# Sixteen visits outside the loop instead of 24, all score maxima inside it, and 24 products held for the end

## The chip, the cores and the metric

The kernel runs on one core of a Trainium2 chip. A core has a matmul engine (TensorE, PE in the profile, with its weight loads as PEld), a vector engine (DVE), an activation engine (ACT), a general engine (POOL) and an engine that mostly issues DMAs (SP). Each works through its own instructions in order; they meet at semaphores. The metric is the device time of one execution in microseconds (us).

## What is computed

The reference mixes an attention block and a token-mixing MLP with a gate for each token. S is 2048 tokens, D is 640, there are 32 heads of 20 that share one key and one value head, and F is 1728.

```python
q, k, v = x @ wq, x @ wk, x @ wv                 # q: 32 heads of 20, k and v: one head of 20
p = softmax(q @ k.T * 20 ** -0.5)                # for each head, over 2048 keys
a = (p @ v, heads side by side) @ wo             # 2048 x 640
b = (gelu(layernorm(x).T @ w1 + b1) @ w2 + b2).T # 2048 x 640
g = sigmoid(x @ gate_w)
out = g * a + (1 - g) * b
```

## The kernel before

**Units.** Queries are cut into 4 blocks of 512 and heads into 8 groups of 4, which gives 32 query tiles, n = 0 to 31. Keys are cut into 16 blocks of 128. One query tile with one key block is a unit, and there are 512 of them, in order of n. A unit has four score products of 128 keys by 512 queries (`qk`, L688), each followed by an exponential on ACT (L700), and then its visit: the four exponentials are multiplied with v into one PSUM bank (`pv_mm`, L721, 32 columns of the array for each head, in two passes, so eight instructions a unit). The array is used as two row halves, b = 0 and b = 1, that run side by side as two lanes: two heads of a unit belong to each half.

**Maxima.** The softmax needs the largest score of each query. For each query tile, 64 further products of 128 queries by 512 keys (`ms_next`, L506, 32 for each half) are reduced to maxima by DVE (L514). When a tile has all 64, DVE merges them (L536), POOL negates and splits them into a high and a low part (L532 to L534), DVE turns them (L541), SP writes them to DRAM (`store_max`, L542), and four DMAs (`fetch_max`, L549, two for each half) put them as two extra rows into the query tile, so that `qk` of that tile subtracts the maximum by itself. The first `qk` of a tile has to wait for these rows. In a step of the loop, `fetch_at` issues them beside the visit of the key block kb = 11 of the tile before.

**The loop.** `n_st` = (512 - TAIL) / 2 = 244 steps. Step j issues, for one half h = j % 2, the eight score products of four units; some maxima (`wants[j]`); on the other half the next batch of other work; and then, as a burst, the visits of units 2j - 2 and 2j - 1. After the burst ACT copies the sum out of its bank (`collect`, L742) and POOL adds it to `osum` (L743). The other work is, in this order, MLP part one, MLP part two, and from step 200 on the output product of a block of 128 tokens (`a_jobs`, L961): for each half of the 640 columns, 5 pieces of the contraction times 3 terms (high by high, low by high, high by low) times 2 row halves, 15 products to a step, four steps to a block. Blocks st = 0 to 10 are done so.

**Scale and store of a query tile.** After its last visit, eight small stages (`norm_steps`, L747) are taken one to a step by `settle`: write the row sums, read them back, reciprocal on DVE (L760), write it (L763), read it back broadcast (four DMAs, L767), scale on POOL (L770), split on POOL (L773, L774), and store the rows to `o_scr` (`put_o`, eight DMAs, L733).

**The tail.** The last 24 units run in 12 stretches (`stretch`), two units each. A stretch has eight score products (four to each half), 16 maxima in all in the first three stretches, and a share of the waiting output products (`tail_job`, L910), in an order found by a random search over a model of the lanes (`best_order`, `trial`); then two visits that add up in one PSUM bank over a whole query tile (`o_bank`), with no collect. The waiting products are all of block 11 (`jobs[0]`, 60 products), the first 384 rows of blocks 12 to 15 (36 products each) and rows 384 to 560 of these (9 for each half of the columns), as a second sum with an addition of its own; three of these eight halves are held (`held`). Each sum ends in a DVE operation that scales by g and adds (L922). Query tile 30 is closed in the tail by `turned_steps` (L784 on).

**The end.** Rows 560 to 640 belong to the heads of query tile 31, which is known only after the last visit. While DVE and ACT normalize it (`last_half`, L812 to L817), PE does the held products with all 128 rows (L1424, 18 of them). Then 24 products with the last 80 rows of wo (`final`, L1402) finish the eight results of blocks 12 to 15, which DVE (L1411) or ACT and POOL (L1414, L1415) scale and add, and two queues store (L1437). The 80 rows of wo come through `last_wo` (a POOL memset, L982, then four DMAs, L985) and `split_last` (POOL).

All DMAs but the last two are issued by SP in program order; an SP instruction that waits holds up those behind it. The same holds for POOL's queue.

Of the kernel before, what the change touches and what calls it, by code (L numbers as in the profile page):

```python
# [10 lines left out]
F32 = mybir.dt.float32  # L11
# [7 lines left out]
P = 128  # L19
# [12 lines left out]
TAIL = 24  # L32
# [7 lines left out]
def mix_kernel(ctx: ExitStack, tc: tile.TileContext, A_x, A_wq, A_wk, A_wv, A_wo,  # L40
# [826 lines left out]
    whole = []  # L867
    tail = [[], []]
    loaded = []
    CUT = 3 * P  # L870
# [5 lines left out]
    def room(i):  # L876
        t, at = (u0, 3 * D * i) if i < 4 else (slot[0], 3 * D * (i - 4))
        return (t[:, at:at + 2 * D].rearrange("p (j c q) -> p j c q", j=2, q=P), f32(t[:, at + 2 * D:at + 3 * D]))

    def tail_load(i):  # L880
        if i < len(jobs):
            st, r0, r1 = jobs[i]
            cols = slice(st * P, (st + 1) * P)
            oT, yt = room(i)
            c0, c1 = r0 // P, r1 // P
            for j in range(2):
                nc.sync.dma_start(out=f32(oT[:, j, c0:c1]),
                                  in_=o_scr[j, r0:c1 * P, cols].rearrange("(c p) s -> p c s", p=P))
                if r1 > c1 * P:
                    nc.sync.dma_start(out=f32(oT[:r1 - c1 * P, j, c1]), in_=o_scr[j, c1 * P:r1, cols])  # L890
            if r0 == 0:
                nc.sync.dma_start(out=yt, in_=y_scr[cols, :])
            loaded.append(i)

    def tail_job(n):
        st, r0, r1 = jobs[n]
        oT, yt = room(n)
        acc, at, ready = {}, {}, []

        def mm(c, k, d, h, first, last):  # L900
            if first:
                i = at[d, h] = busy[h] = next_free()
                while any(k == i for _, k, _ in reduces):
                    reduces.pop(0)[2]()
                acc[d, h] = bank(i)
                free[i] = float("inf")
            o, w = ((oT[:, 0], wo_hi), (oT[:, 1], wo_hi), (oT[:, 0], wo_lo))[k]
            r = slice(64 * h, min(r1 - c * P, 64 * h + 64))
            region = [("x", at[d, h])]
            touch(nc.tensor.matmul(acc[d, h][:, :HD2], o[r, c, :], w[r, c, d * HD2:(d + 1) * HD2],  # L910
                                   start=first, stop=last), writes=region)
            if last:
                ends = lane[h] + 0.15
                while reduces and reduces[0][0] < ends:
                    reduces.pop(0)[2]()
                free[at[d, h]] = spend("dve", 0.48, ends) + 0.24
                sl = slice(d * HD2, (d + 1) * HD2)
                if st not in parts:
                    parts[st] = fin.tile([P, D], F32, name="yo") if r1 == D else spare_row(st)
                add = parts[st] if d in ready or r0 else yt  # L920
                ready.append(d)
                touch(nc.vector.scalar_tensor_tensor(parts[st][:, sl], acc[d, h][:, :HD2], g_col[:, st:st + 1],  # L922
                                                     add[:, sl], op0=ALU.mult, op1=ALU.add), region)
                if len(ready) == 4:
                    if r1 - r0 == D:
                        whole.append(lambda: nc.sync.dma_start(out=y_out[st * P:(st + 1) * P, :], in_=parts[st]))

        for h in range(2):
            ck = [(c, k) for c in range(r0 // P, DC) if r1 - c * P > 64 * h for k in range(3)]
            for d in range(2):  # L930
                if r0 and (st, d) in held:
                    continue
                for i, (c, k) in enumerate(ck):
                    step = lambda a=(c, k, d, h, i == 0, i == len(ck) - 1): mm(*a)
                    tail[h].append((n, ("a" if i == 0 else "e" if i == len(ck) - 1 else "f", step)))
# [104 lines left out]
    aj = [a_jobs(st) for st in range(NS - 5)]  # L1040
# [23 lines left out]
    for i, j in enumerate((221, 241, 242, 243, 243)):  # L1064
        ph[j][1].append(lambda i=i: tail_load(i))
# [131 lines left out]
    for i, (st, r0, _) in enumerate(jobs):  # L1197
        tail_job(i)
# [18 lines left out]
    left, n = 64 * NU - 16 - sum(given) - sum(wants[:at]), n_st - at  # L1217
    wants[at:] = sorted(left * (i + 1) // n - left * i // n for i in range(n))
    assert sum(given) + sum(wants[:n_st - 8]) >= 64 * (NU - 1)
    owed = 0  # L1220
    for j in range(n_st):
# [47 lines left out]
    assert sum(given) == 64 * NU - 16 and not follow  # L1269
# [18 lines left out]
    def trial(kinds, prefer):  # L1288
        line, new, banks_at, held_at = list(lane), list(fresh), list(free), dict(busy)
        dve, act, now, out = clock["dve"], clock["act"], state["at"], []  # L1290
        left = [list(x) for x in kinds]
        while any(left):
            options = []
            for k in range(4):
                if left[k]:
                    at = max(line[k % 2] + W_US * new[k % 2], now)
                    if left[k][0] in "sma":
                        at = max(at, min(banks_at))
                    options.append((at + prefer(k, left), k, at))
            _, k, at = min(options)  # L1300
            kind, h, now = left[k].pop(0), k % 2, at
            new[h] = False
            line[h] = at + (X_US if k < 2 else F_US)
            i = min(range(len(banks_at)), key=lambda i: banks_at[i])
            if kind == "s":
                act = max(act, at + SEEN_US) + EACH["act"][0]
                banks_at[i] = act - EACH["act"][0] + EACH["act"][1]
            elif kind == "m":
                dve = max(dve, at + SEEN_US) + EACH["dve"][0]
                banks_at[i] = dve - EACH["dve"][0] + EACH["dve"][1]  # L1310
            elif kind == "a":
                held_at[h], banks_at[i] = i, float("inf")
            elif kind == "e":
                dve = max(dve, line[h] + 0.15) + 0.48
                banks_at[held_at[h]] = dve + 0.24
            out.append(k)
        end = max(max(line), now + LAST_US - FIRST_US)
        late = sum(max(0.0, t - end - 2.0) for t in banks_at if t < float("inf"))
        return end + 0.3 * late, out

    def best_order(tiles, lanes, i):
# [3 lines left out]
        for _ in range(400):  # L1325
            w = [rng.uniform(-0.4, 0.4) for _ in range(4)]
            z = rng.uniform(0.0, 0.4)
            score = trial(kinds, lambda k, left: w[k] + rng.uniform(0.0, z))
            if best is None or score < best:
                best = score  # L1330
        return best[1]

    busy = {}

    def stretch(i):
# [3 lines left out]
        for b in range(2):  # L1339
# [3 lines left out]
            ms = [("m", ms_next(b)) for _ in range((3, 3, 2)[i] if i < 3 else 0)]  # L1343
            lanes[b] = tail_take(b, math.ceil(len(tail[b]) / (TAIL // 2 - i)))
            tiles[b] = ms + ss if i == 2 else [x for n in range(4) for x in ss[n:n + 1] + ms[n:n + 1]]
# [6 lines left out]
        if i == 2:  # L1352
            for f in ms_done():
                f()
            store_max(NU - 1)
            stores.pop()()
            fetch_max(NU - 1)
        if i > 2 and whole:
            whole.pop()()
        settle()  # L1360
        settle()
        pop_chain()
        if i in (7, 8):
            tail_load(2 * i - 9)
            tail_load(2 * i - 8)
# [12 lines left out]
    assert not tail[0] and not tail[1] and not any(later) and not whole  # L1378
# [80 lines left out]
```

## Time and profile before

| | |
|---|---|
| time, median of 3 runs | 1618.53 us (1618.27 to 1618.7) |
| time of the profiled execution | 1618.5 us |
| its span, first to last instruction | 1616.5 us |
| around the span | 2.0 us |
| mean granted TensorE clock | 0.999 |
| PE busy | 1608.8 us, 100% |
| DVE busy | 1383.9 us, 86% |
| ACT busy | 1261.1 us, 78% |
| POOL busy | 841.1 us, 52% |

Times inside the trace count from the start of the span. A matmul's busy time overlaps with that of its neighbours, so a full PE row does not say that PE is at its peak; the distance between the starts of neighbouring instructions does. A visit shows as a group of L721 instructions, so the distance from one group of 16 to the next is the length of a step or a stretch.

### The profile page before, as it was taken

The page shows a single profiled execution, that of the slowest core. Times are in us where ns is not written, and L with a number is a line of the kernel's source. Part 1 is how long each engine was busy: PE and PEld are TensorE (multiplying, and loading weights), DVE is VectorE, ACT ScalarE, POOL GpSimd, SP SyncE. Part 2 cuts the span into 40 slices and gives each one's busy share as a digit, 9 for nine tenths or more (in the row PEclk, how much of TensorE's full clock was granted, in tenths as well). Part 3 has the DMA queues.
Part 4 walks back from the last instruction along what each step waited for, and adds up shares of the span by engine and source line. Part 5 has one row for each costly group of instructions (what it writes and reads, how often), then busy time and mean ns, then how long its engine had stood idle before and what let it go on. Part 6 is the DMA issues. An engine that isn't in the chain of part 4 may idle for free.

```text
span 1616.5 us, 39520 instructions
## 1 busy us (share of the span) xinstructions
PE 1608.8 (100%) x14868; PEld 1123.3 (69%) x14868; DVE 1383.9 (86%) x2629; ACT 1261.1 (78%) x2350; POOL 841.1 (52%) x927
## 2 busy tenths in 40 slices
PE   9999999999999999999999999999999999999998
PEld 7899876776776776666666666666666666666665
DVE  6689899999999999888888888888888886567754
ACT  4545677777777778878888788887888879999976
POOL 6567766777787776554554334444444433333321
PEclk9999999999999999999999999999999999999999
DMA  7665322232222232222212121112221113333221
GB/s 215 206 168 144 87 66 73 61 77 69 69 70 74 53 76 63 74 68 69 69 47 64 35 61 54 58 54 60 61 60 47 54 37 112 103 115 98 85 83 59
DMA packets 180308, 129.27 MB, mean 80 GB/s; under 512 B 41585, under 2 KB 150030, under 8 KB 180118
## 3 DMA queue, kind: packets, MB, share of 16 engines
q1 hardware_dynamic: 179830, 126.43, 27.7%
q8 instruction: 117, 1.92, 0.5%
q14 instruction: 73, 0.60, 0.1%
q10 hardware_dynamic: 288, 0.33, 0.1%
HBM read 93.57 MB, written 32.15 MB: 78 GB/s over the span
## 4 chain that ended last, share of the span: by engine, by line
PE 98%; POOL 0%; DVE 0%; DMA 0%; issue 0%; ACT 0%; POOLq 0%; SPq 0%; DVEq 0%
PE xs L721 29%; PE xs L688 18%; PE xs L506 18%; PE g L836 11%; PE g L1008 7%; PE pp L302 4%; PE pu L633 4%; PE g L961 3%; PE xs L910 1%; PE x L506 1%; PE pt L294 0%; PE pp L366 0%; PE xs L1424 0%; PE pp L191 0%; PE g L688 0%
## 5 line engine op out<-in xcount | busy, mean ns | idle before, releaser
L514 DVE TENSOR_REDUCE mp<-xs 128x1 f32<-128x512 f32 x1943 | 1196.9, 684 | 154.7 <-PE xs L688 78.4
L700 ACT ACTIVATE p<-xs 128x512 f32<-128x512 f32 (+1 forms) x1834 | 1011.7, 680 | 10.9 <-PE xs L688 6.4
L743 POOL TENSOR_TENSOR osum<-osum,part 128x512 f32<-128x512 f32 x212 | 274.2, 1294 | 604.8 <-ACT part L742 597.9
L721 PE MATMUL xs<-p,v_sb 128*32 128x512 f32 x4096 | 492.3, 598 | 0.0
L688 PE MATMUL xs<-q,kst 62*128 62x512 f32 x1339 | 476.2, 417 | 1.3 <-ACT p L700 1.3
L506 PE MATMUL xs<-kst,q 60*128 60x512 f32 x1242 | 437.4, 416 | 0.0
L688 PEld LDWEIGHTS xs<-q,kst 62*128 62x128 f32 x1339 | 235.9, 185 | 74.6 <-DVE mp L514 52.3
L742 ACT ACTIVATE part<-xs 128x512 f32<-128x512 f32 x212 | 126.8, 598 | 199.6 <-PE xs L721 197.3
L1008 PE MATMUL g<-slot,w 64*128 64x320 f32 x1728 | 266.8, 306 | 0.0
L721 PEld LDWEIGHTS xs<-p,v_sb 128*32 128x32 f32 x4096 | 106.9, 109 | 225.5 <-issue 161.0
L506 PEld LDWEIGHTS xs<-kst,q 60*128 60x128 f32 x1242 | 209.6, 184 | 73.4 <-DVE mp L514 44.4
L1008 PEld LDWEIGHTS g<-slot,w 64*128 64x128 f32 x1728 | 259.1, 184 | 1.9
L127 POOL TENSOR_TENSOR w<-wr,w 128x512 fp32r<-128x512 f32 (+1 forms) x180 | 225.5, 1255 | 34.5 <-ACT w L124 22.1
L688 PE MATMUL xs<-slot,kst 62*128 62x512 f32 x567 | 206.9, 418 | 0.4 <-DVE row L922 0.2
L506 PE MATMUL xs<-kst,slot 60*128 60x512 f32 x573 | 205.3, 418 | 0.0
L836 PE MATMUL g<-u,w 64*128 64x320 f32 x1296 | 201.7, 306 | 0.0
L836 PE MATMUL g<-slot,w 64*128 64x320 f32 x1296 | 201.5, 306 | 0.0
L836 PEld LDWEIGHTS g<-u,w 64*128 64x128 f32 x1296 | 195.6, 184 | 1.7
L836 PEld LDWEIGHTS g<-slot,w 64*128 64x128 f32 x1296 | 195.6, 184 | 1.5
L688 PEld LDWEIGHTS xs<-slot,kst 62*128 62x128 f32 x567 | 99.7, 185 | 31.7 <-DVE mp L514 22.6
L506 PEld LDWEIGHTS xs<-kst,slot 60*128 60x128 f32 x573 | 96.2, 184 | 33.1 <-DVE mp L514 20.4
L961 PE MATMUL g<-slot 64*128 64x320 f32 x660 | 106.7, 306 | 0.0
(197 smaller groups left out, 1483.7 us busy)
## 6 DMA issues: line engine op xcount, KB each, us to landing
wr<-in_B_w_dram SPq DMA_DIRECT2D x155, 256.0 KB
q<-q_scr SPq DMA_DIRECT2D x126, 80.0 KB
rb<-r_scr SPq DMA_DIRECT2D x120, 64.0 KB
slot<-o_scr SPq DMA_DIRECT2D x22, 320.0 KB
y_scr<-yo SPq DMA_DIRECT2D x16, 320.0 KB
q_scr<-qh SPq DMA_DIRECT2D x19, 256.0 KB
q_scr<-ql SPq DMA_DIRECT2D x19, 256.0 KB
o_scr<-rb SPq DMA_DIRECT2D x120, 40.0 KB
```

Source lines behind the costliest of these rows:

```text
L127: nc.gpsimd.tensor_sub(wl, wr, f32(wh))
L302: nc.tensor.matmul(pp, w, t, start=first and n == 0, stop=not more and n == len(steps) - 1)
L506: mm = nc.tensor.matmul(ms, qtiles[n][64 * b:64 * b + 60, pr, qt * P:(qt + 1) * P], kst[64 * b:64 * b + 60, kq * NB:(kq + 1) * NB], start= ...
L514: red = nc.vector.tensor_reduce(out, ms, axis=AX.X, op=ALU.max)
L688: mm = nc.tensor.matmul(s, kst[64 * b:64 * b + 62, kb * P:(kb + 1) * P], q[64 * b:64 * b + 62, pr, :], start=True, stop=True)
L700: act = nc.scalar.activation(p_all[:, a * NB:(j + 1) * NB], s, AF.Exp, scale=SCALE)
L721: mm = nc.tensor.matmul(o[32 * hh:32 * hh + 32, :], v_sb[:, units[u][1], :], p_all[:, j * NB:(j + 1) * NB], start=first, stop=last, skip_g ...
L742: touch(nc.scalar.activation(part, o, AF.Copy), [("x", i)])
L743: nc.gpsimd.tensor_add(osum[n], osum[n], part)
L836: other_tile(half, nc.tensor.matmul(hold["p"][:, :HD2], w[r, fc % HS, :], u[d][r, fc, :], start=(hold["n"] == 1), stop=(hold["n"] == 6 * F ...
L961: other_tile(half, nc.tensor.matmul(hold["p"][:, :HD2], o[r, c, :], w[r, c, d * HD2:(d + 1) * HD2], start=(hold["n"] == 1), stop=(hold["n" ...
L1008: other_tile(half, nc.tensor.matmul(hold["p"][:, :HD2], w[r, st % HS, :], h[d][r, st, :], start=(hold["n"] == 1), stop=(hold["n"] == 6 * NS)))
```

## The change

- TAIL is 16: the loop has 248 steps, the tail 8 stretches. Block 11 becomes a job of the loop.
- All maxima are made in the loop, none in its last three steps. `follow` gets a short cut for the last tile (split and turn in one step, with the store behind), and `fetch_at` fetches its rows beside unit 491, in step 246.
- `last_wo` moves from step 241 to step 246, the last but one, `split_last` to the first stretch.
- Blocks 12 and 13 do rows 0 to 560 in one sum for each half of columns and array. The 48 rows left over from 512 to 560 run on one half alone, block 12 on the lower and block 13 on the upper half, for which two DMAs (`move_wo`, step 240) copy those rows of wo to partitions 64 to 111.
- Blocks 14 and 15 do 384 rows in the tail; both halves of columns of both are held, 24 products, now all with 48 rows first and then all with 128.
- The loads of rows 384 to 560 are issued at the end of stretches 2 and 3 (before: 7 and 8). `settle` runs three times in a stretch (before: twice).
- The order search takes 300 random trials and then 3000 local moves.
- At the end ACT and POOL take two of the eight results and DVE six (before: three and five).

```diff
-TAIL = 24
+TAIL = 16
...
-    jobs = [(NS - 5, 0, D)]
-    jobs += [(st, 0, CUT) for st in range(NS - 4, NS)] + [(st, CUT, HEAD) for st in range(NS - 4, NS)]
-    held = ((NS - 2, 0), (NS - 2, 1), (NS - 1, 0))
+    jobs = [(st, CUT) for st in (NS - 2, NS - 1)] + [(st, HEAD) for st in (NS - 4, NS - 3)]
+    held = tuple((st, d) for st in (NS - 2, NS - 1) for d in range(2))
...
+    def move_wo():
+        for i, w in enumerate((wo_hi, wo_lo)):
+            t = slot[0][:, i * D:(i + 1) * D]
+            nc.sync.dma_start(out=f32(t[64:64 + HEAD - (DC - 1) * P]), in_=f32(w[:HEAD - (DC - 1) * P, DC - 1, :]))
+            low_wo.append(t)
...
-            r = slice(64 * h, min(r1 - c * P, 64 * h + 64))
+            r = slice(64 * h, 64 * h + min(64, r1 - c * P - 64 * h * (c < DC - 1)))
+            w = w[r, c] if h == 0 or c < DC - 1 else low_wo[k // 2][r]
...
-            ck = [(c, k) for c in range(r0 // P, DC) if r1 - c * P > 64 * h for k in range(3)]
+            ck = [(c, k) for c in range(DC) if r1 > c * P and (c < DC - 1 or h == (st == LOW)) for k in range(3)]
...
-    aj = [a_jobs(st) for st in range(NS - 5)]
+    aj = [a_jobs(st) for st in range(NS - 4)]
...
-    for i, j in enumerate((221, 241, 242, 243, 243)):
-        ph[j][1].append(lambda i=i: tail_load(i))
+    for j, (st, _) in zip((241, 242, 243, 244), jobs):
+        ph[j][1].append(lambda st=st: tail_load(st, 0, CUT))
+    ph[n_st - 8][1].append(move_wo)
...
-        if kb == 11 and n + 2 < NU:
+        if kb == 11 and n + 1 < NU:
             fetch_max(n + 1)
...
-    left, n = 64 * NU - 16 - sum(given) - sum(wants[:at]), n_st - at
-    wants[at:] = sorted(left * (i + 1) // n - left * i // n for i in range(n))
+    left, n = 64 * NU - sum(given) - sum(wants[:at]), n_st - 3 - at
+    wants[at:] = sorted(left * (i + 1) // n - left * i // n for i in range(n)) + [0] * 3
...
             follow.pop(0)()
+            if len(row_max) == NU and follow:
+                follow.pop(0)()
+                stores.pop()()
...
-        if j == n_st - 3:
+        if j == n_st - 2:
             raw = last_wo()
-        if j == n_st - 1:
-            w_last = split_last(raw)
...
-        for _ in range(400):
+        for _ in range(300):
...
+        for n in range(3000):
+            order = list(best[1])
+            for _ in range(rng.choice((1, 1, 2, 3))):
+                order.insert(rng.randrange(len(order)), order.pop(rng.randrange(len(order))))
+            score = trial(kinds, order)
+            if score[0] <= best[0]:
+                best = score
...
-            ms = [("m", ms_next(b)) for _ in range((3, 3, 2)[i] if i < 3 else 0)]
...
-        if i in (7, 8):
-            tail_load(2 * i - 9)
-            tail_load(2 * i - 8)
+        if i in (2, 3):
+            for st in range(NS + 2 * i - 8, NS + 2 * i - 6):
+                tail_load(st, CUT, HEAD)
...
-    for st, d in held:
-        oT, _ = room(jobs.index((st, CUT, HEAD)))
-        for c in range(DC - 1, CUT // P - 1, -1):
-            r = min(P, HEAD - c * P)
+    for c in range(DC - 1, CUT // P - 1, -1):
+        r = min(P, HEAD - c * P)
+        for st, d in held:
+            oT, _ = room(st)
...
-                evict(i, d, (i, d) in ((1, 0), (1, 1), (2, 1), (3, 1)))
+                evict(i, d, (i, d) not in ((0, 1), (2, 0)))
```

More of the change, by code (lines that the diff above doesn't have):

```diff
@@ new lines, in tail_load @@
+    def tail_load(st, r0, r1):
+        cols = slice(st * P, (st + 1) * P)
+        oT, yt = room(st)
+        c0, c1 = r0 // P, r1 // P
+        for j in range(2):
+            nc.sync.dma_start(out=f32(oT[:, j, c0:c1]),
+                              in_=o_scr[j, r0:c1 * P, cols].rearrange("(c p) s -> p c s", p=P))
+            if r1 > c1 * P:
+                a = 64 * (st == LOW)
+                nc.sync.dma_start(out=f32(oT[a:a + r1 - c1 * P, j, c1]), in_=o_scr[j, c1 * P:r1, cols])
+        if r0 == 0:
+            nc.sync.dma_start(out=yt, in_=y_scr[cols, :])
+        loaded.append((st, r0))
@@ L895, in tail_job @@
     def tail_job(n):
-        st, r0, r1 = jobs[n]
-        oT, yt = room(n)
+        st, r1 = jobs[n]
+        oT, yt = room(st)
         acc, at, ready = {}, {}, []
@@ L1195, in burst @@
         fresh[:] = [True, True]
-    for i, (st, r0, _) in enumerate(jobs):
+    for i in range(len(jobs)):
         tail_job(i)
@@ L1261, in mix_kernel @@
             new_q(29)
-        if j == n_st - 3:
+        if j == n_st - 2:
             raw = last_wo()
-        if j == n_st - 1:
-            w_last = split_last(raw)
         if j:
             burst((2 * j - 2, 2 * j - 1))
-    assert sum(given) == 64 * NU - 16 and not follow
+    assert sum(given) == 64 * NU and not follow
     xs.append(ps_g.tile([P, NB], F32, name="g"))
@@ L1351, in stretch @@
             stores.pop(0)()
[L1352 to L1362, printed above, removed]
-        if i in (7, 8):
-            tail_load(2 * i - 9)
-            tail_load(2 * i - 8)
+        if i == 0:
+            w_last.extend(split_last(raw))
+        for _ in range(3):
+            settle()
+        if i in (2, 3):
+            for st in range(NS + 2 * i - 8, NS + 2 * i - 6):
+                tail_load(st, CUT, HEAD)
         visits((u0 - 2, u0 - 1))
@@ L1376, in next_acc @@
         return i
-    assert not tail[0] and not tail[1] and not any(later) and not whole
+    assert not tail[0] and not tail[1] and not any(later)
     pool = pools["last"]
```

77 lines of the change are left out of this document (28 added, 49 removed).

## The prediction

> **What bounds the kernel now.** First the page's chain that ended last; then the stretch of time from step 200 to the last visits by windows (columns: time, then busy time and count on PE, PEld, DVE, ACT, POOL, then clock and DMA), for all lines and for the maxima (L506) alone.
>
> ```profile
> PE 98%; POOL 0%; DVE 0%; DMA 0%; issue 0%; ACT 0%; POOLq 0%; SPq 0%; DVEq 0%
> ...
> 1332.79:1452.96 120.17, 120.17 (x1123) 74.99 (x1118) 74.20 (x152) 116.79 (x234) 40.33 (x38) 1.00 0.36 109
> 1452.96:1539.86 86.90, 86.90 (x796) 54.20 (x792) 60.78 (x121) 81.49 (x164) 28.39 (x27) 1.00 0.34 101
> 1539.86:1557.57 17.71, 17.71 (x155) 11.45 (x151) 12.52 (x23) 13.24 (x27) 5.36 (x7) 1.00 0.28 91
> 1557.57:1602.03 44.46, 44.09 (x406) 27.49 (x402) 16.67 (x32) 36.10 (x72) 2.31 (x4) 1.00 0.15 41
> ...
> 1332.79:1452.96 120.17, 39.48 (x104) 17.22 (x104) 1.00 0.36 109
> 1452.96:1539.86 86.90, 28.09 (x90) 13.14 (x90) 1.00 0.34 101
> 1539.86:1557.57 17.71, 6.53 (x16) 2.87 (x16) 1.00 0.28 91
> ```
>
> PE sets the time, at a clock of 1.00. The windows are cut at visits. The first holds steps 200 to 225: 104 / 26 = 4 maxima and 120.17 / 26 = **4.622 us a step**. The second holds steps 226 to 243: 90 / 18 = 5 maxima, **4.828 us a step**. The third is the tail's stretches 0 to 2, 17.71 us with the 16 maxima; the fourth the other nine, 4.94 us each. Together 269.24 us, the part that the change rewrites. What a step consists of shows in the timeline of PE and of ACT:
>
> ```profile
> 1404.70 0.31 PE L961 MATMUL g<-slot 64*128 64x320 f32 x1
> 1404.85 0.45 PE L961 MATMUL g<-slot 64*128 64x320 f32 x2
> 1405.25 0.40 PE L688 MATMUL xs<-slot,kst 62*128 62x512 f32 x1
> 1405.49 0.40 PE L688 MATMUL xs<-slot,kst 62*128 62x512 f32 x1
> 1405.82 1.92 PE L721 MATMUL xs<-p,v_sb 128*32 128x512 f32 x16
> 1407.67 0.73 PE L506 MATMUL xs<-kst,q 60*128 60x512 f32 x2
> ...
> 1407.89 0.60 ACT L742 ACTIVATE part<-xs 128x512 f32<-128x512 f32 x1
> 1408.39 4.02 ACT L700 ACTIVATE p<-xs 128x512 f32<-128x512 f32 x8
> ```
>
> From the start of one visit pair to the first product behind it are 1.85 us; on a lane a 512-wide product follows the last one by 0.24 us, an output product by 0.15; from the last product to the visits pass 0.33. Eight exponentials and a collect take ACT 4.02 + 0.50 = 4.52 us if nothing overlaps.
>
> **Loop and stretches.** 16 maxima move into the loop, which gets one more step with maxima. It now places 104 + 90 + 16 = 210 from step 200 to 244; sorted over 45 steps that is 15 steps of four and 30 of five: 15 x 4.622 + 30 x 4.828 = 214.2 us.
>
> The three steps without maxima have eight scores on one lane and 15 output products on the other. By the PE rows: 1.85, then about 0.25 to the second output product, 13 more at 0.147, then 0.33: 4.34 us. ACT's bound is 4.52 without overlap. Above stands the step with four maxima, 4.62. I take 4.38, nearest to PE's sum, since ACT's successive operations overlap (eight in 4.02 us, while one alone takes about 0.6): 13.1 us. Range 4.34 to 4.62, so -0.1 to +0.7 on the sum.
>
> The tail's products were 60 + 144 + 45 = 249 by the jobs. They become 72 + 108 = 180, 90 on each lane: 12, 12 and then 11 for each of eight stretches. Before, the fuller lane had 132 in 12 stretches, so 11 too, and the other 117. What such stretches cost shows in the chain of waits:
>
> ```profile
> 1566.92 1.90 PE xs L721 x16
> 1568.91 0.70 DVE part L784
> ...
> 1570.27 0.52 DVE row L922
> ...
> 1572.03 1.85 PE xs L721 x16
> ...
> 1576.96 1.85 PE xs L721 x16
> ...
> 1581.81 1.85 PE xs L721 x16
> ...
> 1586.62 1.85 PE xs L721 x16
> ```
>
> 5.11 us for the first, in which DVE closes query tile 30 (L784) ahead of the evictions (L922); then 4.93, 4.85 and 4.81. I take six stretches at 4.84, one with 12 products a lane at 5.0 and one, with tile 30's closing too, at 5.2: 39.2 us. The lane alone (1.85; the first product; three more scores at 0.24 and 11 products at 0.147; 0.33 to the visits) gives about 4.7, and 4.85 with 12: 37.9 at least, and the new order search can win no more than that distance. If every stretch takes 5.11, it is 40.9.
>
> Sum: 214.2 + 13.1 + 39.2 = 266.5, that is **-2.7 us**.
>
> **The rows of maxima for the last tile** are what the plan of the lanes does not see. In the loop `fetch_max` for tile 31 stands on SP behind `last_wo` of the same step 246, whose DMAs wait for a POOL memset, which stands on POOL behind the scaling of query tile 29, which waits for the broadcast rows, whose DMAs stand on SP behind the store of the maxima. The rows for each link, from the timelines of SP, POOL and DVE and from the chain:
>
> ```profile
> 1534.22 1.85 PE xs L721 x16
> 1536.87 1.29 POOL L743 TENSOR_TENSOR osum<-osum,part 128x512 f32<-128x512 f32 x1 [7.71 <-ACT part L742]
> 1557.24 0.26 POOL L532 TENSOR_SCALAR mm<-mm 128x16 f32<-128x16 f32 x1 [4.56 <-DVE mm L536]
> 1558.34 2.51 DMA m_scr<-mt
> 1506.43 1.81 SPq L767 DMA_DIRECT2D rb<-r_scr  x4
> 1545.16 2.55 SPq L767 DMA_DIRECT2D rb<-r_scr  x4
> 1549.35 1.30 POOL L770 TENSOR_TENSOR osum<-osum,rb 128x512 f32<-128x512 f32 x1 [6.35 <-DMA rb<-r_scr]
> 1528.54 0.62 POOL L982 MEMSET yo<- 128x640 f32 x1
> 1531.73 1.48 SPq L985 DMA_DIRECT2D yo<-in_A_wo_dram  x4
> 1560.87 2.75 SPq L549 DMA_DIRECT2D slot<-m_scr  x4
> 1561.60 1.95 DMA slot<-m_scr
> 1577.63 0.61 POOL L796 CAST ot<-part 128x512 fp32r<-128x512 f32 x1 [19.56 <-DVE part L793]
> 1581.26 0.34 SPq L887 DMA_DIRECT2D slot<-o_scr  x1
> ```
>
> Count from the end of step 244's visits. POOL's add ends 0.8 + 1.29 = 2.1 after visits end, split and turn (1557.24 to 1558.34) take 1.1, and an output eviction on DVE ahead of the turn costs up to 0.2 more: store at 3.4. Four broadcast DMAs from 3.8 to 5.6 (1.81; 6.35 by the longer row), landed 1.64 later (1547.71 to 1549.35): 7.2. Scaling to 8.5, memset to 9.2, four DMAs for wo to 10.7, and the four fetches from there. The first half's second fetch starts 0.73 later and lands in 1.95: 13.4. The other half's last starts 2.1 later: 14.8. Stretch 0 wants them after three visits more, at 3 x 4.38 = 13.1. So PE stands 0.3 us if the half that is ready first is scored first and 1.7 if the other is; with the longer broadcast 1.1 and 2.5, and nothing if the whole chain runs 1.7 us faster. I take **+1.0**, between the halves, since the search ignores this wait. Queued behind the waiting score is all of PE, and behind that ACT.
>
> The Trainium skill, "DMA: Bandwidth & Descriptors", Specifications, gives about 0.6 us to the first byte for DMAs issued by SP. Were that the whole wait in place of 1.95, the later half would be there at 13.4, the wait 0.3 at most, and the time about 1615.4. The trace's row is the landing of these very DMAs, so it decides.
>
> The other moved loads I cost at nothing. Rows 384 to 560 of block 12 follow tile 30's store: DVE's closing ends with stretch 1, some 4.9 us after that tile's last visit, and from POOL's first part to the load passed 3.6 us (1577.63 to 1581.26), so they are issued at 8.5 and there at about 12; stretch 3 wants them as its last products, at 2 x 4.9 + 2.6 = 12.4 or later. The cover is the products of blocks 14, 15 and 12's first rows; 2 us later and PE would stand 1.6. `split_last` has the whole tail. The two `move_wo` copies run in step 240 and are wanted from stretch 3 on; they pass SP's queue long before the rows above.
>
> **The end.**
>
> ```profile
> 1604.72 0.44 PEld L1424 LDWEIGHTS xs<-slot,slot 48*128 48x128 f32 x3 [0.84 <-issue]
> 1608.45 1.04 PE L1402 MATMUL xs<-row,q 128*128 128x320 f32 x6
> ...
> 1611.72 0.53 ACT L1414 ACTIVATE p<-xs,g_col 128x320 f32<-128x320 f32 x1 [0.35 <-PE xs L1402]
> 1613.22 0.90 ACTq L1437 DMA_DIRECT2D out_dram<-p  x2
> ```
>
> 18 held products last from 1604.72 to 1608.45, 3.73 us: 0.62 for each triple of one kind, where six final products take (1.04 - 0.31) / 5 = 0.147 each, 0.44 a triple; so each change between 48 and 128 rows costs about 0.18. 24 in two runs of one kind are 24 x 0.147 + 2 x 0.18 = 3.9, so +0.2. The result that went through ACT and POOL and left at 1613.22 now goes through DVE at about 1612.0 and can leave at 1612.6; the last DMA starts some 0.7 to 0.8 earlier. Net **-0.6**, between -0.8 and 0 (if another store ends last).
>
> **Sum.** -2.7 + 1.0 - 0.6 = -2.3. The profiled execution took 1618.5 us (span 1616.5), as good as the median, 1618.53: **1616.2 us**.
>
> **Rivals.**
> *Clean gain.* The chain of the maxima runs as fast as it can, or the ready half is scored first, and the new search fills the lanes better: -2.7 - 0.6 - 0.6 = -3.9, 1614.6 (stretches half way to their bound). For it: the wait hangs on tenths. Against it: POOL and SP are strictly in order, and the stretches shown came no nearer than 0.1 to the lane's bound.
> *Nothing gained.* Stretches take 5.11 because each lane is now full, and steps without maxima take as long as those with four, set by ACT: -2.7 + 1.7 + 0.7 + 1.0 - 0.6 = +0.1, 1618.6. For it: 117 products on the lighter lane left room that is gone. Against it: fewer evictions, 24 for 30.
> *The rows come far too late, slower.* One link, the DMAs of `last_wo` on SP, holds the fetch; the change loses from a wait of 3.3 us on, that is rows at 16.4 and not 14.8. With 4 us more than I count it is 5 us of wait: -3.3 + 5 = +1.7, 1620.2, and from 6.5 us of wait on it is over 0.2%. For it: four broadcast DMAs took 1.81 us once and 2.55 another time, beside the tail's loads. Against it: those loads end with step 244, and seven links would have to slip by half a microsecond each. By the Trainium skill, "TensorE: Matmul & The Clock Gate", Part 1, some 3.4 us without matmuls would also halve the clock, for a window of the same length, some 2 us more; no wait in the windows above is that long, and none shows a clock under 1.00.
>
> **Numbers.** Forecast 0.55, clean gain 0.25, nothing gained 0.12, rows too late 0.08. 0.2% is 3.2 us, what a measurement can tell. Beyond it lie the clean gain and 0.05 of the forecast at its fast edge, so faster 0.30; of the late rows 0.05, so slower 0.05; the rest, 0.65, is the same. Range: from the clean gain with the low bounds, 1614.0, to nothing gained with the longer broadcast's wait, 1619.3.
>
> **What would show it.** Visits 4.62, 4.83 and about 4.4 us apart up to step 247; in stretch 0 a gap on PE of 0.3 to 1.7 us that ends with `slot<-m_scr`, and SP issuing L549 after L985; seven stretches of 4.8 to 5.0; 24 held products in 3.9 us; the last store near 1612.9 less the gain. No gap at all, or one over 3 us, makes the middle wrong; stretches over 5.1 make the first sum wrong.

## The result, and the profile after

The changed kernel takes **1615.51 us** (median of 20 runs, 1614.67 to 1616.98), the kernel before 1618.54 beside it (20 runs, 1617.93 to 1618.94): 3.03 us less, a ratio of 0.9982 (95% interval 0.9976 to 0.9988). The prediction said 1616.2, with 1614.0 to 1619.3 as its range. The forecast was 0.7 us too slow, and the sum hides three misses, of which one has the opposite sign of the other two.

The profiled execution took 1614.67 us, 0.84 less than the median. It was already 0.67 us ahead at step 200, in the part that the change does not touch (the same visits at 1332.12 and not 1332.79), so I compare from step 200 on. From there to the end of the span it is 1612.9 - 1332.12 = 280.8 us, before 1616.5 - 1332.79 = 283.7: 2.9 less, in line with the medians.

The same stretch of time by windows (time, then busy time and count on PE, PEld, DVE, ACT, POOL, then clock and DMA). The windows are the 15 steps of four maxima, the 30 of five, the three without any, stretch 0, stretch 1 and stretches 2 to 7:

```profile
1332.12:1401.50 69.38, 69.38 (x650) 43.24 (x646) 43.01 (x88) 67.12 (x135) 21.80 (x20) 1.00 0.36 110
1401.50:1546.41 144.91, 144.91 (x1324) 90.34 (x1320) 101.94 (x204) 135.65 (x272) 46.01 (x43) 1.00 0.36 108
1546.41:1559.15 12.74, 12.74 (x121) 7.94 (x117) 1.44 (x7) 12.44 (x27) 7.00 (x10) 1.00 0.14 43
1559.15:1564.81 5.66, 5.46 (x52) 3.43 (x48) 1.10 (x2) 5.51 (x12) 4.45 (x4) 1.00 0.38 115
1564.81:1569.87 5.06, 5.06 (x52) 3.20 (x48) 3.67 (x7) 4.45 (x10) 0.28 (x1) 1.00 0.03 8
1569.87:1598.13 28.26, 28.26 (x281) 17.73 (x276) 6.69 (x13) 23.72 (x49) 1.90 (x2) 1.00 0.15 38
```

Together 266.01 us, where before had 269.24: -3.2. PE is still nearly all of the chain that ended last. The steps with maxima cost what they did before: 4.63 and 4.83. Only stretch 0 has PE idle, 5.66 - 5.46 = 0.20 us. By shares of that chain on the page:

```profile
PE 97%; SPq 1%; DVE 1%; issue 0%; POOL 0%; DMA 0%; ACT 0%; DVEq 0%; POOLq 0%
```

The rows of maxima for tile 31, in SP's timeline and then POOL's (start, length, engine, line, operation, operands, count; in brackets the idle time before and what ended it):

```profile
1550.68 0.33 SPq L542 DMA_DIRECT2D m_scr<-mt  x1
1551.11 1.76 SPq L767 DMA_DIRECT2D rb<-r_scr  x4
1556.48 1.41 SPq L986 DMA_DIRECT2D yo<-in_A_wo_dram  x4
1557.94 2.80 SPq L549 DMA_DIRECT2D slot<-m_scr  x4
```

```profile
1554.60 1.28 POOL L770 TENSOR_TENSOR osum<-osum,rb 128x512 f32<-128x512 f32 x1 [0.64 <-DMA rb<-r_scr]
1555.82 0.64 POOL L983 MEMSET yo<- 128x640 f32 x1
```

SP issues nothing from 1552.9 to 1556.48: the loads of wo wait for the memset, that for the scaling, and the fetch (L549) is stuck behind them. PE's timeline shows who pays, and how a step without maxima ends:

```profile
1557.74 0.60 PE L962 MATMUL g<-slot 64*128 64x320 f32 x3
1558.27 1.92 PE L721 MATMUL xs<-p,v_sb 128*32 128x512 f32 x16
...
1560.38 0.30 PE L916 MATMUL xs<-slot,u 64*128 64x320 f32 x1
1560.88 0.47 PE L688 MATMUL xs<-slot,kst 62*128 62x512 f32 x1 [0.20 <-DMA slot<-m_scr]
```

The first score of tile 31 waits for `slot<-m_scr`, and no product starts on either lane between 1560.38 and 1560.88. The search had put three output products ahead of it and a score of the ready half first.

The end, in the timeline of all engines:

```profile
1600.82 0.71 PE L1424 MATMUL xs<-slot,u 48*128 48x320 f32 x3
...
1604.64 2.36 PE L1402 MATMUL xs<-row,q 128*128 128x320 f32 x15
...
1605.89 3.21 SPq L1437 DMA_DIRECT2D out_dram<-p  x6
...
1608.51 1.10 ACTq L1437 DMA_DIRECT2D out_dram<-p  x2
```

The 24 held products take 1604.64 - 1600.82 = 3.82 us (3.73 for 18 before). From the first final product to the end of the span pass 1612.9 - 1604.64 = 8.2 us, where before had 1616.5 - 1608.45 = 8.0. So the end got longer by 0.3 in all, where -0.6 was predicted, although the last two stores start earlier: ACT issues its first one 3.87 us behind the first final product, before 4.77.

### The profile page after: what moved, and what is told of

Its sections match the earlier page's. It is cut to its first block, busy times and chain, and to the rows that moved or that the text cites. A ratio compares the mean times of both kernels' runs of the same rounds, so it can differ in the third digit from the quotient of the medians.

```text
span 1612.9 us, 39517 instructions
## 1 busy us (share of the span) xinstructions
PE 1604.8 (99%) x14865; PEld 1120.8 (69%) x14865; DVE 1378.3 (85%) x2622; ACT 1262.0 (78%) x2353; POOL 845.8 (52%) x930
## 4 chain that ended last, share of the span: by engine, by line
PE 97%; SPq 1%; DVE 1%; issue 0%; POOL 0%; DMA 0%; ACT 0%; DVEq 0%; POOLq 0%
PE xs L721 29%; PE xs L688 18%; PE xs L506 18%; PE g L836 11%; PE g L1009 7%; PE pu L633 4%; PE pp L302 4%; PE g L962 3%; PE x L506 1%; PE xs L916 1%; PE pt L294 0%; DVE st L235 0%; SPq L199 0%; PE xs L1424 0%; DVE mp L514 0%
## 5 line engine op out<-in xcount | busy, mean ns | idle before, releaser
L743 POOL TENSOR_TENSOR osum<-osum,part 128x512 f32<-128x512 f32 x216 | 279.3, 1293 | 617.4 <-ACT part L742 603.7
L962 PE MATMUL g<-slot 64*128 64x320 f32 x720 | 118.2, 306 | 0.0
```

Source lines behind the costliest of these rows:

```text
L743: nc.gpsimd.tensor_add(osum[n], osum[n], part)
L962: other_tile(half, nc.tensor.matmul(hold["p"][:, :HD2], o[r, c, :], w[r, c, d * HD2:(d + 1) * HD2], start=(hold["n"] == 1), stop=(hold["n" ...
```

## The experiments

Each run has its median beside that of the kernel before on the same chip.

| run | median us | before us | what is different |
|---|---|---|---|
| again | 1615.4 | 1618.3 | the changed kernel |
| no_moves | 1615.2 | 1618.3 | order search of before |
| rows_first | 1614.5 | 1618.3 | fetch of the rows ahead of the loads of wo |
| three_by_pool | 1616.3 | 1618.3 | three results of the end on ACT and POOL |
| rows_late | 1615.64 | 1618.72 | fetch asked for one step later |
| rows_mixed | 1616.82 | 1618.72 | held products in the order of before |
| act_block | 1614.52 | 1618.72 | rows_first and 16 small copies on ACT |
| end_order | 1614.42 | 1618.72 | act_block and another order of the results |
| rows_behind | 1621.79 | 1618.68 | fetch behind the eight stores of tile 29 |
| moves_alone | 1617.35 | 1618.68 | kernel before with the new search |
| after_beside | 1615.65 | 1618.6 | the changed kernel |
| best | 1614.74 | 1618.6 | end_order again |

**again**: no edit.

> The changed kernel once more, to see which of its numbers repeat. Median 1615.5 us, 3.0 below the kernel before. Distances of visits: three steps without maxima 4.25 us each, stretch 0 5.66, stretches 2 to 7 4.71 on the mean; 24 held products 3.82 us; from the first final product to the end of the span 8.25. If the late landing of the last store was chance (theory A, an 8 KB fetch of instructions that ran into it), this last number falls to 7.9; if it belongs to the change (theory B), it stays at 8.2 to 8.3.

All of it repeats: 4.24 to 4.25 us for each of the three steps, 5.70 for stretch 0, 4.71 on the mean for stretches 2 to 7, 3.82 for the held products, 8.24 from the first final product to the end of the span. The late end is no chance; it belongs to the change (theory B). What varies between executions is the front: the same visit, two steps behind step 200, came at 1340.5 in the first trace and at 1341.5 in this one.

**no_moves**:

```diff
-        for _ in range(300):
+        for _ in range(400):
...
-        for n in range(3000):
+        for n in range(0):
```

> The changed kernel with the order search of before: 400 random trials, no local moves. Theory A, the local moves brought the stretches from the 4.84 us that I counted to 4.71: stretches 2 to 7 go back to about 4.84, and the time rises by 0.8 to 1.0 us over the changed kernel, to 1616.4. Theory B, the stretches are shorter because 24 evictions are left of 30 and the lanes are full evenly: stretches stay at 4.71 within 0.03, time within 0.3 of 1615.5.

Stretches 2 to 7 by windows:

```profile
1570.49:1598.91 28.42, 28.42 (x281) 17.88 (x276) 7.02 (x13) 23.83 (x49) 1.91 (x2) 1.00 0.15 38
```

28.42 us and not 28.26, 0.03 a stretch; stretch 1 is 0.12 shorter, which takes the rest back. Theory A falls: in the changed kernel the new search is worth nothing that shows (1615.2 beside 1615.4).

**moves_alone**, the other side of it: the kernel before with the 3000 local moves added behind its 400 trials.

> The kernel before with 3000 local moves behind its order search and nothing else of the change. Theory A, the random search alone left the orders of before, with 10 and 11 products on the lanes, away from the lane's bound of 4.62: its stretches 4 to 10, 4.87 on the mean, fall to 4.70 and the time by 1.2 us, to 1617.3. Theory B, the orders are as good as the model of the lanes can make them, as in the changed kernel, where the moves brought 0.03 us in all: within 0.3 of before.

All 12 stretches of the tail by windows, first of the kernel before, then of moves_alone:

```profile
1539.86:1602.03 62.17, 61.80 (x557) 38.94 (x553) 29.19 (x55) 49.34 (x98) 7.67 (x10) 1.00 0.19 55
```

```profile
1539.85:1600.86 61.01, 60.75 (x558) 37.97 (x553) 28.80 (x55) 49.75 (x98) 7.66 (x10) 1.00 0.19 56
```

1.16 us less, and the time falls by 1.3 (ratio 0.9992, 0.9983 to 1.0002, so by the interval alone not quite told from nothing, though all 10 executions lie below all 19 of before). Theory A in the time, but not in the place: 0.48 of the 1.16 lie in the three stretches with maxima (17.71 and 17.23 us), which it did not name, and the last six fall from 4.87 to 4.77 on the mean and not to 4.70. So the order search of before did leave time lying in its own tail, and the changed tail does not need the better one. What makes the new tail easier for 400 random trials (other sums, evenly filled lanes, fewer stretches) was not tried.

**rows_first**:

```diff
-        if j == n_st - 2:
-            raw = last_wo()
         if j:
             burst((2 * j - 2, 2 * j - 1))
+        if j == n_st - 2:
+            raw = last_wo()
```

> The changed kernel with the memset and four loads of wo issued behind the visits of their step, so behind the fetch of tile 31's rows. Theory A, the rows stood behind those loads and cost the longer stretch 0: the wait on the fetched rows goes, stretch 0 falls from 5.66 to about 5.05, time 0.6 lower, 1614.9. Theory B, the length of stretch 0 comes from its 12 products a lane and the wait hides beside ACT: stretch 0 stays at 5.5 or more and the time within 0.2.

SP's timeline, then the windows of stretch 0 and of stretches 2 to 7:

```profile
1551.13 1.77 SPq L767 DMA_DIRECT2D rb<-r_scr  x4
1553.01 2.79 SPq L549 DMA_DIRECT2D slot<-m_scr  x4
1559.04 1.43 SPq L986 DMA_DIRECT2D yo<-in_A_wo_dram  x4
```

```profile
1559.16:1564.31 5.15, 5.15 (x52) 3.22 (x48) 1.10 (x2) 5.15 (x12) 4.43 (x5) 1.00 0.49 157
1569.38:1597.68 28.30, 28.30 (x280) 17.74 (x276) 6.68 (x13) 23.70 (x49) 1.91 (x2) 1.00 0.15 38
```

The fetch goes 4.9 us earlier, PE has no idle time in stretch 0 any more, and stretch 0 is 5.15 us: 0.51 less than in the changed kernel (0.55 by again). The loads of wo come later by 2.6 us, and PE waits for nothing up to the end of the stretches. Theory A, and the price of the wait: 0.5 to 0.6 us by these traces. The median falls by 0.9 (1615.4 to 1614.5); from step 200 to the end of the span the traces show 0.55 of it, and where the rest lies stays open.

**rows_late**:

```diff
-        if kb == 11 and n + 1 < NU:
+        if kb == (13 if n == NU - 2 else 11) and n + 1 < NU:
```

> The changed kernel with the fetch of tile 31's rows one step later, beside unit 493: on SP it then stands behind the store of a block and the eight stores of tile 29, which wait for POOL's split. By the rows of the changed kernel the first half's second fetch is issued at about 1562.7 and lands 2.0 later, at 1564.7, 4.2 us behind its use in the changed kernel. Theory A, the last tile's first score product stands for the rows and everything moves with it: stretch 0 grows by about 4 us, to 9.7, the time to 1619.4. Theory B, part of the wait is taken back because ACT, DVE and POOL catch up in the meantime: stretch 0 at 9.7 but the stretches behind it shorter than 4.71, time 1618.5 or less. Theory C, the clock gate closes after 3.4 us without products and the next 3.4 us run at half speed: time 1621, with a granted clock under 1.00 behind the wait.

Neither theory was tried, because I misread where the fetch would land: the store of a block and the stores of tile 29 are issued by the first stretch and not by the step before it. SP's order stayed the same (L986, then L549), and so did the time. What it shows is small: stretch 0 took 5.82 us, so the same order gives 5.66 to 5.84 over six executions. The fetch starts 0.33 to 0.19 us ahead of the visits in these six, 0.33 in those of 5.66 and 5.74 and 0.25 in that of 5.84, so its start is at most part of the reason.

**rows_behind** does what rows_late should have done:

```diff
-        if kb == 11 and n + 1 < NU:
+        if kb == 11 and n + 2 < NU:
...
         state["f"] = 0.0
+        if i == 0:
+            while stores:
+                stores.pop(0)()
+            settle()
+            fetch_max(NU - 1)
```

> The changed kernel with the fetch of tile 31's rows moved behind three things of SP's queue: the loads of wo, the store of a block and the eight stores of tile 29, which wait for POOL's split. By the rows of the changed kernel the stores end at about 1562.4, the first half's second fetch is issued at 1563.1 and lands 2.0 later, at 1565.2, where the changed kernel's first score product of that tile stood ready at 1560.1. Theory A, the score products stand for the rows and everything moves with them: stretch 0 about 10.2 us (5.15 without a wait and 5.0 of it), time 1615.5 - 0.6 + 5.0 = 1619.9. Theory B, what ACT was behind is worked off in the wait, so stretch 0 is 9.8 or less and the time 1619.5. Theory C, the clock gate: products stand for more than 3.4 us, so the next 3.4 us run at half clock: stretch 0 at 11.5 or more, a granted clock under 1.00 in it, time 1621 or more.

SP's timeline, PE's waits (waiting line, what it waited for, us, times, longest), and windows around the wait (the last column but two is the granted clock):

```profile
1561.68 1.40 SPq L733 DMA_DIRECT2D o_scr<-osum  x4
1563.12 2.80 SPq L549 DMA_DIRECT2D slot<-m_scr  x4
```

```profile
PE xs L688 <- DMA slot<-m_scr: 4.6, 1, 4.6
```

```profile
1557.43:1560.13 2.70, 2.70 (x29) 1.84 (x30) 0.55 (x2) 2.70 (x7) 2.23 (x3) 1.00 0.31 82
1561.36:1565.96 4.60, 0.00 (x1) 0.03 (x2) 0.00 (x0) 0.72 (x2) 3.45 (x3) 0.85 0.31 76
1565.96:1569.40 3.44, 3.44 (x23) 3.44 (x25) 0.63 (x2) 1.79 (x3) 0.00 (x0) 0.50 0.02 2
1569.40:1572.84 3.44, 3.44 (x25) 1.25 (x23) 0.47 (x1) 2.55 (x5) 0.00 (x0) 0.70 0.00 0
1572.84:1577.08 4.24, 4.24 (x45) 3.05 (x44) 3.68 (x7) 3.57 (x8) 0.00 (x0) 1.00 0.00 0
```

The score products stand for 4.60 us, and **the 3.44 us behind the wait run at a granted clock of 0.50**. If the clock is either 1.00 or 0.50, the means 0.85 and 0.70 say that it fell 3.2 us into the wait and rose 5.5 us after its end. The median lies 3.1 us over before (ratio 1.0019, 1.001 to 1.0028), where the changed kernel is 3.0 under: 6.1 us for a wait that is 4.4 us longer (4.60 for 0.20 us of idle PE). Theory C. The wait of the changed kernel leaves the clock at 1.00. The Trainium skill, "TensorE: Matmul & The Clock Gate", Part 1, has the clock halve after about 3.4 us without work, in windows that run on regardless of the kernel, and come back after a window of work. The trace agrees on the fall; the return took longer than one window, which windows that do not start with the work would allow.

**three_by_pool**:

```diff
-                evict(i, d, (i, d) not in ((0, 1), (2, 0)))
+                evict(i, d, (i, d) not in ((0, 1), (2, 0), (3, 0)))
```

> The changed kernel with result (3,0) of the end on ACT and POOL again, so three and five as before. Theory A, as predicted: the result leaves 0.6 later and the end moves with it, first final product to end of span 8.25 + 0.6 = 8.85, time 1616.1. Theory B, the eight stores of 160 KB run through the DMA engines back to back at about 0.49 us each from the second on, so an earlier issue of the last two only makes them queue: first final to end 7.9 to 8.3, time within 0.3 of 1615.5.

ACT's timeline, and the DMA queues between 1609.6 and 1610.1 (packets, MB, share):

```profile
1608.29 0.53 ACT L1414 ACTIVATE p<-xs,g_col 128x320 f32<-128x320 f32 x1 [0.35 <-PE xs L1402]
1609.78 1.88 ACTq L1437 DMA_DIRECT2D out_dram<-p  x2
```

```profile
q1 hardware_dynamic: 143, 0.16, 90.1%
q14 instruction: 1, 0.01, 3.9%
```

The end is 1614.0 - 1605.01 = 9.0 us behind the first final product: 0.77 longer, where theory A has 0.6. But this is not theory A's reason. The kernel before sends its results the same three and five ways and needs 8.0. The difference is in the two issues of ACT: 1.88 us here, 0.90 before. The first of them alone took 1.40 us and not 0.38, and an instruction fetch (q14; by the page 74 such packets with 0.61 MB, 8 KB each) starts 0.1 us ahead of it, at 1609.67. So this run does not tell what the result itself costs on ACT and POOL; the kernel before and act_block (below), neither with a fetch there, do: 8.0 and 7.7, that is 0.3.

**act_block** (with rows_first):

```diff
     for i in range(TAIL // 2):
         stretch(i)
+    for i in range(16):
+        nc.scalar.activation(idle[:, i:i + 1], g_col[:1, :1], AF.Copy)
```

> The version with the rows' fetch ahead of the loads of wo (1614.5) and 16 copies of one number on ACT between the last exponentials and the last normalizing, where ACT stood idle for 3.7 us. They move an 8 KB fetch of ACT's instructions, which came 6.1 us after the first final product and ran beside the last stores, to a place ahead of them. Theory A, this fetch holds up packets of the last two stores: the last landing comes at 6.9 after the first final product and not at 7.36, the span's end at 7.8 and not 8.24, time 1614.1. Theory B, the two ACT stores and SP's last simply share the DMA engines: 8.2 and 1614.5 as without the copies.

The DMA view from the first final product to the end (GB/s in 40 slices, then the fetch's queue, where there is a fetch), of the kernel before, of the changed kernel, and of act_block, and then ACT's timeline of act_block (its lines stand three further down):

```profile
GB/s 0 0 0 0 0 0 0 0 0 0 134 376 293 13 38 325 351 268 351 319 325 357 306 344 319 344 363 70 261 351 249 351 344 77 0 0 0 0 0 0
```

```profile
GB/s 0 0 0 0 0 0 0 0 0 0 230 379 187 0 130 373 305 336 360 299 348 286 360 367 336 373 330 348 379 363 261 31 12 12 0 0 0 0 0 0
...
q14 instruction: 1, 0.01, 0.2%
```

```profile
GB/s 0 0 0 0 0 0 0 0 0 0 7 320 380 147 0 120 366 313 293 366 287 366 340 287 366 360 360 353 353 366 340 360 340 33 0 0 0 0 0 0
```

```profile
1598.75 1.59 ACT L1372 ACTIVATE idle<-g_col 1x1 f32<-1x1 f32 x16
...
1608.35 0.87 ACTq L1440 DMA_DIRECT2D out_dram<-p  x2
```

In the changed kernel an 8 KB fetch lies between the stores, the last two stores trail off (31, 12, 12 GB/s in the last three slices of 0.2 us), and ACT needs 1.10 us for its two issues. With 16 instructions more on ACT ahead of it the fetch comes at 1596.6, ACT needs 0.87, no slice trails off, and the end is 1612.16 - 1604.47 = 7.7 us behind the first final product: **0.54 less** than in the changed kernel and in rows_first (8.24 in both), theory A. The fetch takes 0.31 us from 6.09 on; the last packet of the stores ends at 6.91 with it and at 6.47 without. ACT's second issue is also 0.29 us earlier in act_block (4.35 for 4.64), but the packets of that store begin to flow at about 5.8 in both. One instruction more on ACT (three_by_pool) brought the fetch to just ahead of the first issue; sixteen bring it ahead of all; in the kernel before none came until the span was over. By the pages ACT has 2350 instructions before, 2353 in the changed kernel, 2354 in three_by_pool and 2369 in act_block. So what the change added to ACT's program pushed a fetch into the last stores. The median of act_block, 4.2 under before where rows_first is 3.8 under, has room for this half microsecond but does not prove it. The traces do: all eight with the fetch at 6.1 end at 8.24 or 8.25, the three with the copies (act_block, end_order, best) at 7.6 to 7.7. The Trainium skill, "Runtime: NRT & Kernel Launch", Instruction fetch mechanics, says that crossing a block of instructions is mostly hidden. In the middle of the kernel nothing measured here speaks against it; at the end of this one it cost 0.54, and about 1.0 in three_by_pool (9.0 against 8.0 in the kernel before).

The same rows show the second thing that the prediction left out. From about 3.0 us on the stores of the changed kernel and of act_block run at some 290 to 380 GB/s without a break. Seven stores of 160 KB at some 340 GB/s are 3.4 us, so the last is not through before about 6.4, however early it is issued.

**end_order** (with act_block), and **best**, which is the same kernel beside **after_beside**, the changed one:

```diff
-            if (i, d) == (0, 0):
-                evict(i, d, True)
-                turn[1][5]()
-            else:
-                evict(i, d, (i, d) not in ((0, 1), (2, 0)))
+            evict(i, d, (i, d) not in ((1, 0), (2, 0)))
+            if (i, d) == (0, 1):
+                turn[1][5]()
```

> As act_block, and at the end results (1,0) and (2,0) go through ACT and POOL and not (0,1) and (2,0); DVE does (0,1) before the last subtraction of the normalizing; SP stores (0,0), (0,1), (1,1), (1,0), (2,1), (2,0). The second store can then leave at 1.7 after the first final product and not at 2.13. Theory A, the stores run through the DMA engines at 0.49 us each from the second on, so an earlier second store ends all of them earlier: end of span 0.3 to 0.45 earlier than act_block, time 0.3 to 0.45 lower. Theory B, the last result sets the end, at 4.3 as before: same time within 0.15.

> The changed kernel, on one chip with the version of end_order. Median 3.0 us under before; span 0.3 to 1 us above its best execution. The late last landing repeats: 8.24 us from the first final product to the end of the span.

> The version of end_order beside the changed kernel on one chip. Theory A, the three edits add as their traces said, 0.55 for the rows, 0.54 for the fetch of instructions, 0.06 for the order of the results: 1.1 us under the changed kernel and 4.1 under before. Theory B, the medians of act_block and rows_first, equal at 1614.5, say that the end's half microsecond does not show in the time: 0.6 to 0.9 under the changed kernel.

DMA view of best from the first final product to the end:

```profile
GB/s 0 0 0 0 0 0 0 0 0 0 0 302 349 282 383 336 68 40 316 370 229 356 323 316 336 336 383 343 383 343 350 356 336 47 0 0 0 0 0 0
```

The second store now follows the first without a gap, but the gap has only moved behind it, to the third, since the third result is as late as it was. The end is 7.64 us behind the first final product in end_order (7.63 in best), 0.06 less than in act_block where 0.3 to 0.45 were expected; theory A had the rate right and overlooked the third result. best takes 1614.74 us beside 1615.65 for the changed kernel and 1618.6 for before: -0.9 and -3.9 (ratio to before 0.9975, 0.9966 to 0.9985). By the traces from step 200 on it is 1.2 under the changed kernel; the median shows 0.9, and nothing tells the two apart. No version here is faster.

**rows_mixed**:

```diff
-    for c in range(DC - 1, CUT // P - 1, -1):
-        r = min(P, HEAD - c * P)
-        for st, d in held:
-            oT, _ = room(st)
+    for st, d in held:
+        oT, _ = room(st)
+        for c in range(DC - 1, CUT // P - 1, -1):
+            r = min(P, HEAD - c * P)
```

> The changed kernel with its 24 held products in the order of before, for each result 48 rows and then 128, so seven changes of the number of rows and not one. Theory A, a change costs about 0.2 us as I read from 18 products in 3.73: the held products take 24 x 0.147 + 7 x 0.2 + 0.1 = 5.0 and not 3.82, and the end moves by 1.2: time 1616.6. Theory B, the held products wait for nothing and something else sets when the final products start (DVE's normalizing): the end moves by less than 0.5.

PE's timeline:

```profile
1602.64 1.34 PE L1424 MATMUL xs<-slot,u 48*128 48x320 f32 x6
...
1607.63 1.62 PE L1402 MATMUL xs<-row,q 128*128 128x320 f32 x10
```

4.99 us for the held products and not 3.82, and the end behind them as long as before (8.24): the time rises by 1.2. Theory A: with seven changes of the number of rows in place of one the products take 1.17 us more, 0.2 for each of the six that came on top.

## Why the prediction was near, point by point

- **Steps with maxima**: 214.2 us predicted, 69.38 + 144.91 = 214.3 measured. Right.
- **Three steps without maxima**: 4.38 each, 13.1; measured 4.25, 12.74. Under the lower bound, and the row shows why: I let the visits follow the last product by 0.33 us, as they follow a score. Here the last one is an output product (three from 1557.74 at 0.147, the last at 1558.03), and the visits begin at 1558.27, 0.24 behind it. ACT does not hold them either, as its timeline shows:

```profile
1551.90 0.69 ACT L742 ACTIVATE part<-xs 128x512 f32<-128x512 f32 x1
1552.38 4.13 ACT L700 ACTIVATE p<-xs 128x512 f32<-128x512 f32 x8
1556.20 0.80 ACT L742 ACTIVATE part<-xs 128x512 f32<-128x512 f32 x1
...
1560.49 0.92 ACT L742 ACTIVATE part<-xs 128x512 f32<-128x512 f32 x1
```

  Eight exponentials and a collect start 4.30 us apart, so ACT's bound was 4.30 and not 4.52; three such steps put ACT some 0.15 us behind PE.
- **Stretches**: six at 4.84 were predicted, 4.71 measured (28.26 / 6), which is the bound of about 4.7 that the prediction worked out for the lane alone. The one with 12 products was put at 5.0 and the one with tile 30's closing at 5.2; rows_first has 5.15 and 5.07. The term for the six was mis-sized by 0.8 us: I took it from stretches of the kernel before (4.93, 4.85, 4.81) that fall by 0.1 to 0.2 with a better order (4.76, 4.67, 4.72 in moves_alone). Of the clean gain's reasons, the new search fell with no_moves.
- **The rows of maxima**: every link came where it was counted (step 244's visits end at 1547.4; from there the store 3.3 us, 3.4 predicted; memset done 9.1, 9.2 predicted; fetch 10.6, 10.7 predicted). The wait was +1.0 in the sum and measured 0.5 to 0.6 by rows_first. The choice "between the halves" was the miss: the half fetched first was scored first (its second fetch starts at 1558.71, which with the row's 1.95 lands at 1560.7, and the score runs at 1560.88), and the row for that, 0.3, was the nearer one.
- **The end**: -0.6 predicted, +0.3 measured. The held products were right (3.9 predicted, 3.82). The earlier issue came too: ACT's second store, the last DMA, starts 5.24 us behind the first final product before, 4.64 in the changed kernel and 4.35 in act_block (0.7 to 0.8 earlier was predicted). The step that failed is "the last DMA starts some 0.7 to 0.8 earlier" as a gain at the end: its issue is not its landing. The stores queue in the DMA engines, which leaves -0.3 (8.0 to 7.7 by act_block), and the fetch of ACT's instructions adds 0.54.
- **Sum**: loop and stretches -3.7 (269.24 to 266.01, with the wait's 0.5 taken out) where -2.7 was said, the wait +0.5 for +1.0, the end +0.3 for -0.6: -2.9 in place of -2.3. That the total lies so near is in part luck: misses of -1.5 and of +0.9 all but cancel. The low end of the range does not come out of its own terms (-2.7, -1.3 for stretches at 37.9, -0.1 and -0.6 give 1613.8 and not 1614.0); nothing hangs on it.
- **The slow rival** was never near: it needed the fetch behind the stores too. Built as rows_behind it cost 6.1 us for 4.4 us of wait, 1.7 more; the prediction's sentence on the clock had some 2 us more.

## What to carry to other kernels

When a load is moved, read the whole queue that issues it at its new place: here exchanging two statements in the program, and so the loads and the fetch on SP, was worth 0.5 us, where the order search brought the changed kernel nothing. A step's length is the distance between starts of the instructions that really end it, so take the row of the kind that will stand last, not of the kind that stood last. At the end of a kernel an earlier issue gains only what the DMA engines have free, and there even the position of an instruction fetch shows.

## What the runs showed of the hardware

- Where a fetch of 8 KB of instructions started 0.1 us ahead of ACT's issue of a DMA, that issue took 1.40 us and not 0.38 (one trace); beside the last stores a fetch delayed the end by 0.54. Where it falls depends on how many instructions ACT's program has.
- Stores of 160 KB ran at 286 to 373 GB/s while SP's queue ran alone and at 330 to 379 while ACT's ran beside it (changed kernel, slices of 0.2 us): a second queue brought next to nothing.
- After 4.6 us without products the granted clock was 0.50 for 3.4 us and more (rows_behind); in the changed kernel, with 0.20 us of idle PE, it stayed at 1.00.
- A change between held products of 48 and of 128 rows cost 0.2 us (1.17 us for six more of them in rows_mixed).
